# A new order table for a hand-planned attention, FFT and FFN kernel on one core

## The chip, the cores and the metric

The kernel runs on one core of a Trainium2 chip. Its engines are TensorE (PE; its weight loads stand apart as PEld), VectorE (DVE), ScalarE (ACT), GpSimd (POOL) and SyncE (SP), which here issues nearly all DMAs. The metric is device time in microseconds, the median over runs.

## The reference

```python
scores = scale * np.matmul(q, k.transpose(0, 1, 3, 2))      # B, H, S, D = 8, 8, 576, 64
mask = (rel >= 0) & (rel < 64)
scores = np.where(mask, scores, -1000000000.0)
attn = softmax(scores)                                      # over the last axis
x = (attn @ v), heads side by side                          # B, 576, 512
mixed = np.real(np.fft.fft(np.fft.fft(x, axis=1), axis=2))
u = x + mixed
un = (u - mean) / np.sqrt(var + 1e-06)
out = u + np.maximum(un @ w_ch1, 0.0) @ w_ch2               # 512 -> 2048 -> 512
```

All inputs and both weights are drawn in numpy; the weights arrive in 64-bit floats.

## The kernel before

The 4608 rows are cut into 36 tiles `T` of 128 rows. Tiles 0 to 10 do attention in fp32 (`whole`), the later ones in pairs of fp16 numbers, high and low part, with three products in place of one (`PASSES`). For each tile there is one score step (L652, into `psc`, 64 by 64 blocks of TensorE, 32 matmuls in fp32 and 48 of 128 columns in fp16) and two steps for attention times values (`av`, L729, into `pa`, blocks of 128 by 64, one for each half `g` of the heads). All other matmuls use the whole array of 128 by 128, or nearly all of it. VectorE masks the scores (L667), ScalarE takes the exponentials (L675), GpSimd or VectorE inverts the sums (L742, L744), VectorE scales the result (L748).

For each of the 8 batches a Fourier transform follows (`flip_y` L832, `dstage` L972, `sstage` L1006); its rows go to DRAM and are fetched again, tile by tile, by an indirect DMA (`gather`, into `mt`). `norm_tile` adds, normalises and turns the tile.

The FFN works on 18 chunks `c` of two tiles. Chunk 0 runs in fp32 while the weights are still being converted (three VectorE instructions a piece, L1219, L1224, L1231; 32 pieces). Chunks 1 to 13 have 16 first steps (`one`, L1330, 12 matmuls of 256 columns into `ph`) and 16 second steps (`go`, called second step below, L1311, 6 matmuls of 512 columns into `po`); between them ScalarE makes the high part `hh` (L1339) and VectorE the low part (L1342). Chunks 14 to 17 use a scheme with seven products in place of eight (`ffn7`, L1484 and L1459); the last one ends with `direct` (L1471).

Nothing is scheduled by a compiler. Each piece of work is registered as an `Op` in a `Plan`, which numbers them from 0 to 3200. `ORDER` is a table of these numbers, written out; the ops are emitted in that order, and each engine, and SP's queue of DMAs too, runs its own in the order in which they were emitted. `SECOND` lists the ops that go to their second engine where there is a choice of two. `Plan.follow` walks the table with modelled durations. What of that walk reaches the chip is the engine of each op and the length of the modelled gaps: ahead of FFN chunk 0, a TensorE gap over `WARM[0]` is filled with matmuls on nothing (`warm`, L1658), to keep its clock up:

```python
if early and o.eng == "PE" and gap > WARM[0]:
    for _ in range(int((gap - WARM[1]) / 0.21)):
        nc.tensor.matmul(warm, wide[:, 0:P], wide, start=True, stop=True)
```

Of the 8 banks of PSUM, `ph` has a ring of two, `po` has one of two, and a ring of four (`ps`) serves the scores (two banks a step), `av` (one a step), the turns and the stages of the transform.

Of the kernel before, what the change touches and what calls it, by code (L numbers as in the profile page):

```python
# [48 lines left out]
SLACK = 0.5  # L49
PLAIN = 1  # L50
WSC, PSC = 1.1, 1.0
# [222 lines left out]


class Op:
    __slots__ = ("eng", "dur", "lat", "fn", "deps", "outs", "prio", "wait", "ready", "allocs", "bufs", "idx", "durs", "margin", "port", "slack")


class Plan:  # L280
# [16 lines left out]
    def op(self, eng, dur, prio, fn, reads=(), writes=(), lat=0.0, alt=(), holds=(), port=True):  # L297
# [3 lines left out]
        o = Op()  # L301
# [5 lines left out]
        deps = set()  # L307
# [85 lines left out]
def attn_fft_ffn_kernel(ctx: ExitStack, tc: tile.TileContext, q, k, v, w1, w2, gidx, dft_d, dft_s, mask, out):  # L393
# [1040 lines left out]
    def ffn7(c):  # L1434
# [145 lines left out]
        if end:  # L1580
# [18 lines left out]
            for k, n in enumerate((2, 3)):  # L1599
                w, z = slice(CH * k, CH * k + CH), Buf()  # L1600
                o = op("DVE", 0.36, -11, lambda n=n, k=k: add(x_(0)[:, k], n, x_(0)[:, k]), [bpo[2], Bosc, ba], [z], port=False)
                if k == 0:
                    o.deps.discard(right_half)
# [86 lines left out]
```

## Time and profile before

| | |
|---|---|
| median of 3 runs | 971.66 us |
| lowest and highest | 968.44 and 972.33 us |
| the profiled execution | 967.56 us |
| its span, first to last instruction | 965.8 us |
| TensorE busy | 941.5 us, 97% |
| VectorE, ScalarE, GpSimd busy | 688.9, 427.3 and 455.7 us |
| mean granted TensorE clock | 1.000 |

TensorE's busy time is the union of the matmuls' spans from start to modelled end. A 512-column matmul is shown with 380 ns, though the next one can start well before that; so the pace of TensorE is read from starts, not from busy time.

### The profile page before, as it was taken

Reading aid. Unit: us, or ns where it says so; the run is one execution under the profiler, and the core shown is the slowest. Engines: PE = TensorE matmul, PEld = TensorE weight load, DVE = VectorE, ACT = ScalarE, POOL = GpSimd, SP = SyncE. Lnnn points to the kernel's source line nnn. Section 1 sums busy time; section 2 is a strip of 40 time slices with the busy share of each in tenths; the row PEclk is TensorE's granted clock in tenths of the full one; section 3 lists DMA queues with packets and bytes.
Section 4 is the critical chain, followed back from the end, with each engine's and each line's share of the span. In section 5 each row is a group of like instructions: output and inputs, shape, how many; then the busy total and the mean of one; then the engine's idle time right before and its main releaser. Section 6 shows DMA issues by size and latency. Waiting matters only on the chain.

```text
span 965.8 us, 24609 instructions
## 1 busy us (share of the span) xinstructions
PE 941.5 (97%) x9646; PEld 688.5 (71%) x9646; DVE 688.9 (71%) x1940; ACT 427.3 (44%) x1010; POOL 455.7 (47%) x866
## 2 busy tenths in 40 slices
PE   7889999999999999999999999999999999999998
PEld 5666767666676677666676667766576668888887
DVE  6998998886866676666655765666588998566645
ACT  5876676655443524442334333343343634223311
POOL 3664342474663343866734435364863524333251
PEclk9999999999999999999999999999999999999999
DMA  9986734779779765896566855586543511101101
GB/s 234 224 234 195 208 98 108 126 138 184 135 137 164 121 116 130 166 164 105 116 128 140 154 116 107 127 169 127 95 106 89 118 23 37 44 12 45 45 1 67
DMA packets 293892, 117.14 MB, mean 121 GB/s; under 512 B 277064, under 2 KB 277448, under 8 KB 293776
## 3 DMA queue, kind: packets, MB, share of 16 engines
q1 hardware_dynamic: 290912, 106.52, 52.9%
q0 software_dynamic: 2720, 8.92, 3.3%
q8 instruction: 76, 1.25, 0.6%
q14 instruction: 40, 0.33, 0.1%
q10 hardware_dynamic: 144, 0.13, 0.0%
HBM read 54.99 MB, written 14.17 MB: 72 GB/s over the span
## 4 chain that ended last, share of the span: by engine, by line
PE 74%; DMA 9%; DVE 8%; POOL 5%; issue 2%; ACT 1%; SPq 1%; DVEq 0%; POOLq 0%; ACTq 0%
PE po L1311 24%; PE ph L1330 23%; PE ph L1484 9%; PE po L1459 7%; PE pa L729 3%; PE pz L1006 2%; PE pg L972 2%; DMA py<-yp 2%; DMA uhl<-up 2%; PE psc L652 2%; DMA mt<-md,gix 2%; DVE pr L667 1%; POOL flex L508 1%; DMA qn<-in_q 1%; POOL y L508 1%
## 5 line engine op out<-in xcount | busy, mean ns | idle before, releaser
L1311 PE MATMUL po<-w1s,hh 128*128 128x512 f16 (+1 forms) x1312 | 334.9, 391 | 1.9 <-DVE hh L1342 1.9
L1330 PE MATMUL ph<-uhl,w0s 128*128 128x256 f16 (+1 forms) x2616 | 331.9, 278 | 2.6 <-DVE hh L1342 2.4
L1330 PEld LDWEIGHTS <-w0s 128*128 128x128 f16 x2496 | 241.7, 98 | 62.4 <-issue 3.9
L1311 PEld LDWEIGHTS <-hh 128*128 128x128 f16 x1248 | 117.7, 98 | 107.5 <-DVE hh L1342 4.2
L1339 ACT ACTIVATE hh<-ph 128x512 f16<-128x512 f32 x104 | 61.6, 592 | 146.4 <-PE ph L1330 119.1
L1342 DVE SCALAR_TENSOR_TENSOR hh<-ph,hh 128x512 f16<-128x512 f32 x104 | 71.3, 686 | 45.3 <-ACT hh L1339 44.9
L675 ACT ACTIVATE pr<-pr,nm 128x128 f32<-128x128 f32 x288 | 90.8, 390 | 27.9 <-DVE nm L667 26.6
L742 POOL TENSOR_TENSOR rc<-rc,mone 128x4 f32<-128x4 f32 x43 | 49.7, 1158 | 104.4 <-ACT rc L735 56.6
L1484 PE MATMUL ph<-uhl,w0s 128*128 128x256 f16 x768 | 90.2, 273 | 0.0
L1484 PEld LDWEIGHTS <-w0s 128*128 128x128 f16 x768 | 75.0, 98 | 9.5
L1080 POOL DMA_INDIRECT mt<-md,gix x34 | 40.5, 1193 | 75.9 <-DVE mv L1108 55.4
L667 DVE CUSTOM_DVE_ANT_0 pr<-psc,mskb 128x128 f32<-128x128 f32 x288 | 64.9, 285 | 10.5 <-PE psc L652 10.1
L508 POOL TENSOR_TENSOR flex<-pr,flex 128x128 f16<-128x128 f32 x92 | 45.6, 524 | 23.1 <-ACT flex L498 16.8
L1495 ACT ACTIVATE hx<-ph 128x512 f32<-128x512 f32 x31 | 18.4, 597 | 68.2 <-PE ph L1484 52.7
L1459 PEld LDWEIGHTS <-hh 128*128 128x128 f16 x434 | 42.4, 98 | 4.9
L729 PE MATMUL pa<-ve,pt 128*64 128x65 f16 (+1 forms) x776 | 42.4, 204 | 3.0 <-ACT pt L498 1.2
L1508 POOL TENSOR_TENSOR hl<-hx,hh 128x256 f16<-128x256 f32 (+1 forms) x40 | 25.8, 674 | 41.0 <-ACT hh L498 22.2
L508 POOL TENSOR_TENSOR up<-un,up 128x128 f16<-128x128 f32 x60 | 28.4, 502 | 31.2 <-ACT up L498 21.2
L729 PE MATMUL pa<-va,pt 128*64 128x65 f16 (+1 forms) x776 | 42.4, 204 | 0.0
L508 POOL TENSOR_TENSOR y<-xu 128x128 f32<-128x128 f32 x76 | 37.6, 524 | 9.9 <-DVE xu L748 6.6
L1105 DVE CUSTOM_DVE_ANT_0 xu<-xu,mt 128x511 f32<-128x511 f32 (+6 forms) x50 | 35.2, 703 | 9.5 <-DMA mt<-md,gix 9.3
L1115 ACT ACTIVATE un<-xu,mv 128x512 f32<-128x512 f32 x34 | 24.4, 717 | 36.1 <-DVE mv L1108 26.7
(229 smaller groups left out, 1633.4 us busy)
## 6 DMA issues: line engine op xcount, KB each, us to landing
wd<-in_moe_w_ch SPq DMA_DIRECT2D x20, 512.0 KB
out<-xu SPq DMA_DIRECT2D x35, 256.0 KB
kn<-in_k SPq DMA_DIRECT2D x32, 256.0 KB
qn<-in_q SPq DMA_DIRECT2D x32, 256.0 KB
flex<-in_moe_w_ch SPq DMA_DIRECT2D x12, 512.0 KB
ve<-va SPq DMA_DIRECT2D x47, 130.0 KB
flex<-in_v SPq DMA_DIRECT2D x22, 256.0 KB
md<-mp SPq DMA_DIRECT2D x24, 192.0 KB
```

The source lines that it names most:

```text
L508: eng.tensor_tensor(out=out[:, k : k + w], in0=in0[:, k : k + w], in1=in1[:, k : k + w], op=al)
L667: nc.vector.tensor_tensor_reduce(out=t["pr", g][:, hp], in0=t["ps", g][:, hp], in1=mskb[:, m : m + P], scale=-0.125, scalar=3.0e38, op0=AL ...
L675: nc.scalar.activation(pr, pr, AF.Exp, bias=t["nm", g][:, hp : hp + 1], scale=-1.0)
L729: nc.tensor.matmul(pa[sl, hp], pt[:, sl], v_, start=(x == 0), stop=(x == len(mm) - 1))
L742: eng.tensor_tensor(out=rc, in0=rc, in1=mone, op=ALU.pow)
L1080: nc.gpsimd.indirect_dma_start(out=mts[T], out_offset=None, in_=mds[pb][0 : HR if n < 4 else 2 * HR], in_offset=bass.IndirectOffsetOnAxis( ...
L1311: nc.tensor.matmul(t["po"][i], l_, r_, start=(f == 0 and x == 0), stop=(f == NKF - 1 and x == len(mm) - 1))
L1330: nc.tensor.matmul(ph, l_, r_, start=(x == 0), stop=(x == len(mm) - 1))
L1339: nc.scalar.activation(t["hh", j][:, 0], ph, AF.Relu)
L1342: nc.vector.scalar_tensor_tensor(out=hh[:, 1], in0=ph, scalar=0.0, in1=hh[:, 0], op0=ALU.max, op1=ALU.subtract)
L1459: nc.tensor.matmul(t["po", bk][:, x], t["h", j][a][:, slot], right(n, j, b_), start=(j == 0 and k == 0 and n in opens), stop=(j == seven - ...
L1484: nc.tensor.matmul(ph, l_, r_, start=(x == 0), stop=(x == len(mm) - 1))
```

## The change

`ORDER` and `SECOND` are replaced; both tables were made with other settings of the plan. The plan's op gets a `mode` (2 for the score step, 1 for `av`, 0 for all else), and where the mode of a TensorE op differs from that of the one before it, `MODE` = 0.1 us is added to its modelled time. The modelled times of the score and `av` steps are changed. FFN chunks 1 to 13 are planned with `FSLACK`, which assumes that what they wait for comes later than modelled, by 0.4 times the `LATE` of the producer's engine. One dependency that had been dropped by hand in the last chunk (the first half of the last sum against `right_half`) is kept again. No op is added, removed or altered in what it computes. The opening stretch of the new table, which is the attention up to FFN chunk 0 and a little beyond, follows an older order: it starts with the loads of keys and queries, and the weight pieces come later in SP's queue.

```diff
-SLACK = 0.5
+SLACK, FSLACK = 0.5, 0.4
...
-WSC, PSC = 1.1, 1.0
+WSC, PSC = 0.95, 0.7
...
 ORDER = [int(i) for i in """
-11 171 172 3 16 1 0 10 2 7 9 12 13 14 174 175 176 177 180 185 8 186 187 17 181 182 200 18 203 204 188 201 205 206 183
...
+    MODE = 0.1
...
-        o.port, o.slack = port, self.slack
+        o.port, o.slack, o.mode = port, self.slack, mode
...
-        port = 0.0
+        port, mode = 0.0, 0
...
-                end = self.pe_time(busy, st, o.dur)
+                end = self.pe_time(busy, st, o.dur + (self.MODE if o.mode != mode else 0.0))
+                mode = o.mode
...
-        op("PE", WSC if whole else PSC, base + 2, lambda: score((0, 1)), rd, [*bss, *bps])
+        op("PE", WSC if whole else PSC, base + 2, lambda: score((0, 1)), rd, [*bss, *bps], mode=2)
...
-            op("PE", 0.63 if whole else 0.5, base + 6 + 0.5 * g, av, rd, [bpa, bx] if g == 0 else [bpa])
+            op("PE", 0.65 if whole else 0.43, base + 6 + 0.5 * g, av, rd, [bpa, bx] if g == 0 else [bpa], mode=1)
...
-                right_half = op("PE", 0.66, pr + 13.2, lambda: direct(0, 1), rd, [bpo[2]])
+                op("PE", 0.66, pr + 13.2, lambda: direct(0, 1), rd, [bpo[2]])
...
-                if k == 0:
-                    o.deps.discard(right_half)
...
-    plan.slack = 0.0
+    plan.slack = FSLACK
     for c in range(PLAIN, SEVEN):
         ffn(c)
```

## Rows read from the trace of the kernel before

**Rows 1.** The page: granted TensorE clock in 40 slices of the span, in tenths.
```profile
PEclk9999999999999999999999999999999999999999
```

**Rows 2.** Busy time of each engine in four stretches; the second number is their length.
```profile
0.00:97.00 97.00, 82.54 (x964) 61.31 (x965) 81.27 (x287) 68.35 (x180) 49.80 (x97) 1.00 0.84 221
97.00:157.00 60.00, 60.00 (x416) 41.57 (x415) 54.26 (x135) 43.28 (x110) 21.85 (x40) 1.00 0.57 148
157.00:788.00 631.00, 625.36 (x6675) 433.19 (x6674) 441.79 (x1272) 267.57 (x636) 321.72 (x626) 1.00 0.65 128
788.00:965.80 177.80, 173.60 (x1597) 152.39 (x1595) 111.62 (x248) 48.10 (x88) 62.31 (x106) 1.00 0.12 34
```

**Rows 3.** TensorE's waits from 157 us on: us in total, times, longest.
```profile
PE ph L1330 <- DVE hh L1342: 2.4, 3, 1.0
PE po L1311 <- DVE hh L1342: 1.9, 3, 0.8
PE pa L729 <- DMA pt<-flex: 0.9, 3, 0.3
```

**Rows 4.** Timeline of TensorE around one `av` step: start, us, what.
```profile
399.92 1.48 PE L1330 MATMUL ph<-uhl,w0s 128*128 128x256 f16 x12
401.23 1.46 PE L1311 MATMUL po<-w1s,hh 128*128 128x512 f16 x6
402.62 0.22 PE L729 MATMUL pa<-ve,pt 128*64 128x65 f16 x1
...
402.99 0.20 PE L729 MATMUL pa<-ve,pt 128*64 128x65 f16 x1
...
403.13 1.47 PE L1311 MATMUL po<-w1s,hh 128*128 128x512 f16 x6
404.43 0.82 PE L1330 MATMUL ph<-uhl,w0s 128*128 128x256 f16 x6
```

**Rows 5.** Timeline of TensorE around a score step among FFN steps.
```profile
433.38 0.86 PE L652 MATMUL psc<-kst,qbd 64*64 64x128 f16 x48
434.18 0.39 PE L1311 MATMUL po<-w1s,hh 128*128 128x512 f16 x1
```

**Rows 6.** Timeline of TensorE around a score step with an `av` step behind it.
```profile
460.94 0.86 PE L652 MATMUL psc<-kst,qbd 64*64 64x128 f16 x48
461.74 0.22 PE L729 MATMUL pa<-ve,pt 128*64 128x65 f16 x1
...
462.24 0.61 PE L1311 MATMUL po<-w1s,hh 128*128 128x512 f16 x2
```

**Rows 7.** Busy time of the filling matmuls (L1658) in the opening: TensorE, weight loads.
```profile
0.00:97.00 97.00, 14.33 (x84) 8.88 (x84) 1.00 0.84 221
```

**Rows 8.** The chain that ended last, one link near the opening's end: start, us.
```profile
83.72 6.69 DMA mt<-md,gix
```

**Rows 9.** VectorE's groups up to 97 us: busy us, mean ns, idle before.
```profile
L1224 DVE SCALAR_TENSOR_TENSOR w0s<-wd,w0s 128x512 int32<-128x512 int32 x9 | 6.5, 722 | 0.2
...
L1219 DVE TENSOR_SCALAR w0s<-wd 128x512 int32<-128x512 int32 x9 | 6.0, 680 | 4.9 <-DMA wd<-in_moe_w_ch 4.9
...
L744 DVE RECIPROCAL rc<-rc 128x4 f32<-128x4 f32 x6 | 1.1, 176 | 0.2
```

**Rows 10.** The page's group of GpSimd's inverses.
```profile
L742 POOL TENSOR_TENSOR rc<-rc,mone 128x4 f32<-128x4 f32 x43 | 49.7, 1158 | 104.4 <-ACT rc L735 56.6
```

**Rows 11.** Timeline of TensorE around one wait of a second step.
```profile
698.84 0.59 PE L1311 MATMUL po<-w1s,hh 128*128 128x512 f16 x2
700.24 1.04 PE L1311 MATMUL po<-w1s,hh 128*128 128x512 f16 x4 [0.81 <-DVE hh L1342]
```

**Rows 12.** Timeline of VectorE near the end.
```profile
959.73 0.69 DVE L508 TENSOR_TENSOR xu<-xu,s 128x512 f32<-128x512 f32 x1
...
960.53 0.88 DVE L1559 SCALAR_TENSOR_TENSOR xu<-po,osc,xu 128x256 f32<-128x256 f32 x2
```

More of the change, by code (lines that the diff above doesn't have):

```diff
@@ L276 @@
 class Op:
-    __slots__ = ("eng", "dur", "lat", "fn", "deps", "outs", "prio", "wait", "ready", "allocs", "bufs", "idx", "durs", "margin", "port", "slack")
+    __slots__ = ("eng", "dur", "lat", "fn", "deps", "outs", "prio", "wait", "ready", "allocs", "bufs", "idx", "durs", "margin", "port", "slack", "mode")
 class Plan:
@@ L295, in __init__, with op @@
         self.slack = 0.0
-    def op(self, eng, dur, prio, fn, reads=(), writes=(), lat=0.0, alt=(), holds=(), port=True):
+    def op(self, eng, dur, prio, fn, reads=(), writes=(), lat=0.0, alt=(), holds=(), port=True, mode=0):
         o = Op()
         o.durs = {e: d + self.FIXED[e] for e, d in ([(eng, dur), alt[:2]] if alt else [(eng, dur)])}
-        o.port, o.slack = port, self.slack
+        o.port, o.slack, o.mode = port, self.slack, mode
         o.margin = alt[2] if len(alt) > 2 else self.MARGIN
@@ L1600, in ffn7 @@
                 w, z = slice(CH * k, CH * k + CH), Buf()
-                o = op("DVE", 0.36, -11, lambda n=n, k=k: add(x_(0)[:, k], n, x_(0)[:, k]), [bpo[2], Bosc, ba], [z], port=False)
-                if k == 0:
-                    o.deps.discard(right_half)
+                op("DVE", 0.36, -11, lambda n=n, k=k: add(x_(0)[:, k], n, x_(0)[:, k]), [bpo[2], Bosc, ba], [z], port=False)
                 put = lambda e, w=w: e.dma_start(of[P * 2 * c : P * (2 * c + 1), w], xts[2 * c][:, w])
```

277 rows, old and new, of tables (ORDER, SECOND) are left out of this document.

## Prediction

> **What bounds the kernel now.** I read the clock first, then busy time by stretch, then the waits, and last the timeline around single steps. The granted clock is 1.00 in every slice, the upper of the two levels [rows 1], so clock plays no part. The stretches [rows 2] part the run in two. Up to 97 us TensorE is idle for 97 − 82.5 = 14.5 us and fills 84 matmuls on nothing [rows 7]; at the pace of a 256-column matmul, 1.31 us for twelve or 0.109 us each [rows 4], these are 9.2 us, so at least 23.7 us of the opening hold none of the kernel's products. VectorE is busy for 81.3 of 97 us there and the DMA engines for 0.84 of it: the opening is bound by supply. From 97 us on TensorE is idle for 5.6 us until 788 and for 4.2 us after it, and the last of these is the final result's way out. Each matmul there starts when the one before lets it: six of 512 columns take 404.43 − 403.13 = 1.30 us, 0.217 each [rows 4]. So past 97 us only three things can make the kernel shorter: fewer matmuls (none is removed), fewer late starts, and less time lost between matmuls of different block shape.
>
> That loss is the point of the change, and busy time hides it; starts show it. In [rows 4] six second-step matmuls begin at 401.23, and at 0.217 the next one is due at 402.53. It is an `av` matmul and starts at 402.62: 0.09 us lost on entry. The twelve pairs of `av` start every 0.034 us (402.62 to 402.99 in eleven steps), so a follower would be due at 403.02; the next second step starts at 403.13: 0.11 us lost on leaving. The score step alone takes 434.18 − 433.38 = 0.80 us to its follower [rows 5]. With an `av` step right behind it takes the same, 461.74 − 460.94 = 0.80, and that `av` step 462.24 − 461.74 = 0.50, as after an FFN step, where it takes 0.51 [rows 4, 6]. So a direct change from score to `av` costs what leaving to full blocks costs, and saves the entry.
>
> **The changes of shape, counted.** I resolved both tables into TensorE's 781 ops and counted neighbours of unlike mode: 199 before, 143 after. Up to the first step of FFN chunk 1 there are 48 and 46, which I leave at nothing: supply covers them there. Behind it there are 151 and 97. Before, 75 blocks of narrow work (49 of one `av`, 24 of one score, one pair of `av`, one score with `av`); after, 41 (11 pairs of `av`, 10 scores alone, 10 of two `av` and a score, 5 single `av`, 5 score with one `av`). Of narrow blocks that is 34 less: 34 entries at 0.09 = 3.1 us, 34 exits at 0.105 = 3.6 us gained, and 14 more direct changes at 0.10 = 1.4 us lost: 5.3 us gained in all. Seven of the 15 direct changes go from `av` to score, which no undisturbed row shows. From below they could cost nothing (+0.7 us gain), from above an exit and an entry, 0.20 (−0.7 us). I take 0.10, as for the other direction, and keep 4.6 to 6.0. As TensorE streams without pause there, the whole sum should reach the end.
>
> [...]
>
> **Settings of the plan.** `MODE`, `FSLACK`, and the modelled durations reach the chip only through the tables and the number of fillers. The fillers lie before FFN chunk 0, where they use time in which TensorE waits anyway; a wrong number costs 0.109 each when the wait is shorter than planned. I count nothing, and for ten more or fewer ±1 us, which goes into the opening's bounds.
>
> **Late starts behind 157 us,** where FFN chunk 1 begins. TensorE's waits on `hh` are 4.3 us in six, on the turned probabilities 0.9 us in three [rows 3]. The idle time is counted from a modelled end: in [rows 11] the third matmul was due at 698.84 + 2 × 0.217 = 699.27 and came at 700.24, 0.97 us late where 0.81 is shown. With 0.16 more for each of nine the loss is 6.6 us. The new table assumes `hh` to come 0.4 × 0.5 = 0.2 us later, so the same six events would cost 1.2 us less. The shortest distance of TensorE work between an FFN first step and the second step that reads it rises from 1.7 to 2.0 us. Against it: by my count along the tables, places where a PSUM bank of `ps` is taken again within 4 us of TensorE work after its last filling rise from 1 to 7, and first steps with one step of 1.3 us between them and the user of their bank from 1 to 4; that first one was not late before. As all other starts are drawn anew I take 1.0 us gained, with bounds of 4 us either way: 4 is most of the 6.6, and as much again could come up.
>
> **The opening.** Two things move. First, keys and queries go ahead of the first weight piece in SP's queue (which becomes the seventh DMA). The first score step can then start earlier, but VectorE, which sits idle for 4.9 us until that piece lands [rows 9], does its three conversions, about 2 us at 0.7 each, later. I set one against the other. Second, what VectorE has in its queue ahead of the normalised second tile, which opens the FFN: 41 weight conversions before, 37 after, at 0.72 us each [rows 9] 2.9 us less. But six more inverses are on VectorE ahead of it, at 0.18 us [rows 9] 1.1 us. Net 1.8 us, of which I take 1.4 as VectorE is busy for 81.3 of 97 us [rows 2]. DMAs issued ahead of the FFN are as many. The link that ends the opening, a gather of 6.7 us [rows 8], hangs on SP's queue, which I can't follow to the microsecond: bounds 4 us earlier, 4 us later.
>
> **The end.** The dependency kept again lets the first half of the last sum wait for `right_half`. In the trace that sum starts at 960.53, and VectorE was busy with the add before it until 960.42 [rows 12], so the freedom gave nothing, and I count nothing; if that add were gone, it would cost one half sum, 0.4 us.
>
> **Sum.** 5.3 + 1.0 + 1.4 = 7.7 us off the profiled execution's 967.56, 959.9. That execution lies 4.1 us below the median of 971.66, so for a median 964.0.
>
> **The rivals.**
> - *The opening gives it back (no change).* The older order puts the weight pieces six or more DMAs later. If FFN chunk 0 or the gather behind it comes 6 us later, 5.3 + 1.0 − 6 leaves 971.4. For it: the opening is bound by supply, DMA share 0.84 [rows 2]. Against: the conversions ahead of the FFN are fewer. 0.23.
> - *Narrow blocks wait for banks (slower).* Two `av` steps and a score take all four banks of `ps`; the following user of `ps` waits until a bank is read, and all of TensorE behind it. A bank of `av` is held by an inverse of 1.16 us on GpSimd [rows 10] and the scaling behind it. From 0.13 us for each of the 41 blocks the 5.3 us are gone; from (7.7 + 4.9)/41 = 0.31 us the kernel is slower by 0.5%. At 0.4 us, 16.4 − 7.7 = 8.7 us, 980.4. Against: the waits behind 157 us are on `hh` and on the turned probabilities, none on the reading of a bank of scores or of `av` [rows 3]. 0.09. [...]
> - *The new order suits the chip better in all three parts.* Late starts fall by 4 us and the opening by 4: 971.7 − 13.3 = 958.4. 0.13.
> - *Merged steps keep part of the loss.* Each step, not each block, may pay its run-out, so that only the entries are saved: 3.1 + 2.4 = 5.5 us, 966.2. For it: no undisturbed row shows two `av` steps in a row. Against: the twelve pairs inside a step pay nothing [rows 4]. 0.03.
>
> **How the numbers follow.** The forecast has 0.52. Within it the bounds of each part, not all at one end, give 960.5 to 968. What a measurement of this kernel can tell from no change is about 0.5%, 4.9 us, so "faster" is below 966.8: 0.45 of the forecast's 0.52, 0.13 of the third rival, 0.02 of the last, 0.60. Slower: the bank rival, with 0.01 of a worse opening, 0.10. The rest, 0.30, is the same. The range reaches from 957 (all good bounds) to 971.5 (the opening gives it back); what lies beyond is below 0.2.
>
> **What would show it.** In the profile after: blocks of two or three narrow steps in TensorE's timeline, the entry and exit still 0.09 and 0.11; no matmul more or less in L652, L729, L1330, L1311; waits on `hh` at or below 4.3 us; the first fp16 first step of chunk 1 some 1.4 us earlier than now, and from there to the last matmul about 6 us less. I am wrong if a direct change from `av` to score costs far more than 0.2, if waits on PSUM banks or on the turned probabilities show up behind the blocks, or if chunk 1 starts several us later than in the trace of before.

## The result and the profile after

| | before | after |
|---|---|---|
| median (4 runs each) | 970.17 us | 957.97 us |
| lowest and highest | 968.44 and 972.33 us | 954.84 and 959.15 us |
| the profiled execution | 967.56 us | 959.15 us |
| its span | 965.8 us | 957.4 us |

The ratio is 0.9868, with a 95% interval of 0.9834 to 0.9902: faster, by 12.2 us between the medians and by 8.4 us between the profiled executions. Three of the four times before are those of the table ahead of the prediction. The execution profiled before lies below all four, and the one profiled after is the highest of its four, so the two traces show less of the gain than the medians do.

The page of the new kernel, busy time of each engine and the granted clock in 40 slices:

```profile
PE 931.4 (97%) x9638; PEld 689.9 (72%) x9638; DVE 692.5 (72%) x1960; ACT 431.5 (45%) x1013; POOL 446.9 (47%) x835
...
PEclk9999999999999999999999999999999999999999
```

The granted clock is at 0.9 or more in every slice, as in [rows 1], and 1.00 in each stretch below, as in [rows 2]; it has no part in the difference. Busy time of each engine in the stretches of [rows 2]; the second number is their length:

```profile
0.00:97.00 97.00, 82.21 (x1001) 63.64 (x1002) 82.30 (x302) 71.01 (x180) 47.14 (x92) 1.00 0.84 223
97.00:157.00 60.00, 60.00 (x412) 42.34 (x408) 54.64 (x135) 43.06 (x112) 27.42 (x48) 1.00 0.55 147
157.00:788.00 631.00, 624.89 (x6713) 438.62 (x6712) 451.34 (x1286) 266.13 (x636) 316.35 (x605) 1.00 0.65 128
788.00:957.40 169.40, 164.29 (x1524) 145.26 (x1522) 104.25 (x240) 51.30 (x87) 55.96 (x91) 1.00 0.13 36
```

Beside [rows 2] the reader sees no busy share move: 624.89 for 625.36 us of the long stretch. What moved is how much was done in it: 6713 matmuls for 6675 there, 1001 for 964 up to 97 us, though the opening has fewer fillers, 76 for the 84 of [rows 7]:

```profile
0.00:97.00 97.00, 12.93 (x76) 8.10 (x76) 1.00 0.84 223
```

TensorE's waits from 157 us on (us in total, times, longest), as [rows 3] of before:

```profile
PE po L1313 <- DVE hh L1344: 1.8, 1, 1.8
PE pa L731 <- DVE nm L669: 0.8, 1, 0.8
PE py L834 <- DVE y L510: 0.7, 1, 0.7
PE ph L1332 <- DVE hh L1344: 0.7, 1, 0.7
PE pz L1008 <- DVE g L984: 0.6, 1, 0.6
PE pa L731 <- DVE xu L750: 0.5, 1, 0.5
```

The waits on `hh` fell from 4.3 to 2.5 us. Two of the others are new in kind: `av` waits for VectorE to mask scores (`nm`) or to scale an earlier `av` (`xu`). `av` reads neither; it needs a bank of the ring `ps` that they are still reading. The timeline of TensorE shows these waits, and the blocks:

```profile
153.87 1.47 PE L1332 MATMUL ph<-uhl,w0s 128*128 128x256 f16 x12
...
321.18 0.86 PE L654 MATMUL psc<-kst,qbd 64*64 64x128 f16 x48
321.97 0.22 PE L731 MATMUL pa<-ve,pt 128*64 128x65 f16 x1
...
323.09 0.19 PE L731 MATMUL pa<-ve,pt 128*64 128x65 f16 x1 [0.55 <-DVE xu L750]
...
502.31 1.04 PE L1332 MATMUL ph<-uhl,w0s 128*128 128x256 f16 x8
503.27 0.86 PE L654 MATMUL psc<-kst,qbd 64*64 64x128 f16 x48
504.07 0.22 PE L731 MATMUL pa<-ve,pt 128*64 128x65 f16 x1
...
504.82 0.19 PE L731 MATMUL pa<-ve,pt 128*64 128x65 f16 x1
504.95 0.82 PE L1313 MATMUL po<-w1s,hh 128*128 128x512 f16 x3
...
526.87 0.86 PE L654 MATMUL psc<-kst,qbd 64*64 64x128 f16 x48
528.53 0.22 PE L731 MATMUL pa<-ve,pt 128*64 128x65 f16 x1 [0.79 <-DVE nm L669]
...
721.76 0.19 PE L731 MATMUL pa<-ve,pt 128*64 128x65 f16 x1
721.88 0.86 PE L654 MATMUL psc<-kst,qbd 64*64 64x128 f16 x48
```

The block at 503.27 is the change at its best: a score step, then two `av` steps. The eight matmuls ahead are due to end their turn at 502.31 + 8 × 0.109 = 503.18, and the score comes at 503.27: 0.09 lost on entry. It takes 0.80 to its follower, as in [rows 5, 6]. The 24 pairs of both `av` steps start in 504.82 − 504.07 = 0.75 us, 0.033 apart, so the second step of the two pays nothing; the exit takes 0.13, of which 0.10 is loss. At 721.76 the one direction that before didn't show, `av` to score, takes 0.12 from start to start where 0.03 is usual: 0.09 lost. At 321.97 and 526.87 the same kind of block is held up, once by a bank of `av`, once by a bank of scores.

VectorE at both ends of the run (the first row is the first masking, at 9.74 us before):

```profile
8.47 0.29 DVE L669 CUSTOM_DVE_ANT_0 pr<-psc,mskb 128x128 f32<-128x128 f32 x1 [2.36 <-PE psc L654]
...
951.13 0.88 DVE L1561 SCALAR_TENSOR_TENSOR xu<-po,osc,xu 128x256 f32<-128x256 f32 x2 [0.84 <-PE po L1473]
...
952.49 0.75 DVE L1576 SCALAR_TENSOR_TENSOR xu<-po,osc,xu 128x512 f32<-128x512 f32 x1 [0.49 <-PE po L1473]
```

The last half sums wait for the matmuls (0.84 us) and no longer stand behind an add, as in [rows 12].

**Where the 8.4 us came from.** For each pair of matmuls that follow each other I took the distance of their starts and subtracted the usual distance for the first one's shape. At a change of shape what is left over, up to 0.14 us, is the change's loss and more is a late start; elsewhere what exceeds 0.1 us is one. "Products" is the sum of the usual distances, and "rest" holds gaps below 0.1 us and the time to the first matmul. By that, up to the start of the last matmul (961.22 us before, 952.01 after):

```
                       before   after   difference
products               893.5    893.5      0.0
fillers                  9.2      8.3     -0.9
changes of shape        22.1     16.5     -5.6
late starts, to 210 us  23.5     21.7     -1.8
late starts behind       7.3      8.0     +0.7
rest                     5.6      4.0     -1.6
from there to the end    4.55     5.36    +0.8
```

Chunk 1's first step starts at 153.87 for 156.81 us, 2.9 earlier; from it to the last matmul 798.1 us pass for 804.4, 6.3 less. About 0.9 us of that is work which moved: eight turns of keys that stood behind chunk 0's start now stand ahead of it, and about as much, most of it of a transform, moved from behind chunk 1's start to ahead of it. Behind chunk 1's start the 151 changes took 16.2 us, the 97 take 10.6: 0.107 and 0.109 each.

### The profile page after: what moved, and what is told of

Its sections match the earlier page's. It is cut to its first block, busy times and chain, and to the rows that moved or that the text cites. A ratio compares the mean times of both kernels' runs of the same rounds, so it can differ in the third digit from the quotient of the medians.

```text
span 957.4 us, 24610 instructions
## 1 busy us (share of the span) xinstructions
PE 931.4 (97%) x9638; PEld 689.9 (72%) x9638; DVE 692.5 (72%) x1960; ACT 431.5 (45%) x1013; POOL 446.9 (47%) x835
## 4 chain that ended last, share of the span: by engine, by line
PE 83%; DVE 5%; DMA 4%; POOL 4%; issue 2%; ACT 1%; SPq 0%; POOLq 0%; DVEq 0%; ACTq 0%
PE ph L1332 28%; PE po L1313 27%; PE ph L1486 9%; PE po L1461 7%; PE pa L731 3%; PE pz L1008 2%; PE psc L654 2%; PE pg L974 2%; DMA qn<-in_q 2%; POOL h L510 1%; DVE y L510 1%; PE py L834 1%; DMA flex<-in_v 1%; PE mt L1051 1%; POOL flex L510 1%
## 5 line engine op out<-in xcount | busy, mean ns | idle before, releaser
L1313 PEld LDWEIGHTS <-hh 128*128 128x128 f16 x1248 | 119.8, 98 | 107.4 <-DVE hh L1344 2.8
L1082 POOL DMA_INDIRECT mt<-md,gix x34 | 38.4, 1128 | 80.1 <-DVE mv L1110 41.0
L744 POOL TENSOR_TENSOR rc<-rc,mone 128x4 f32<-128x4 f32 x38 | 43.6, 1152 | 53.8 <-ACT rc L737 51.4
L510 POOL TENSOR_TENSOR up<-un,up 128x128 f16<-128x128 f32 x76 | 35.8, 501 | 48.0 <-ACT up L500 37.6
L1502 DVE TENSOR_TENSOR hx<-hx 128x128 f32<-128x128 f32 x104 | 28.0, 312 | 31.9 <-ACT hx L1497 30.9
L510 POOL TENSOR_TENSOR flex<-kn,flex 128x128 f16<-128x128 f32 x72 | 36.8, 540 | 29.9 <-ACT flex L500 27.0
L1461 PEld LDWEIGHTS <-hh 128*128 128x128 f16 x434 | 42.5, 98 | 4.9
L731 PE MATMUL pa<-ve,pt 128*64 128x65 f16 (+1 forms) x776 | 39.0, 203 | 4.3 <-ACT pt L500 1.9
L510 POOL TENSOR_TENSOR flex<-qn,flex 128x128 f16<-128x128 f32 x76 | 34.5, 483 | 16.9 <-ACT flex L500 8.2
L510 POOL TENSOR_TENSOR flex<-pr,flex 128x128 f16<-128x128 f32 x68 | 34.6, 538 | 14.8 <-ACT flex L500 8.6
```

Of the source, the lines that this page charges most:

```text
L510: eng.tensor_tensor(out=out[:, k : k + w], in0=in0[:, k : k + w], in1=in1[:, k : k + w], op=al)
L731: nc.tensor.matmul(pa[sl, hp], pt[:, sl], v_, start=(x == 0), stop=(x == len(mm) - 1))
L744: eng.tensor_tensor(out=rc, in0=rc, in1=mone, op=ALU.pow)
L1082: nc.gpsimd.indirect_dma_start(out=mts[T], out_offset=None, in_=mds[pb][0 : HR if n < 4 else 2 * HR], in_offset=bass.IndirectOffsetOnAxis( ...
L1313: nc.tensor.matmul(t["po"][i], l_, r_, start=(f == 0 and x == 0), stop=(f == NKF - 1 and x == len(mm) - 1))
L1461: nc.tensor.matmul(t["po", bk][:, x], t["h", j][a][:, slot], right(n, j, b_), start=(j == 0 and k == 0 and n in opens), stop=(j == seven - ...
```

## The experiments

An edit of the table is written as a rule on lists; OLD and NEW are the two tables, and of `SECOND` each op keeps the choice of the table that it comes from. All ratios are to the kernel before on the same chip, with a 95% interval.

### One opening with the other rest

The cut lies at the first step of chunk 1 (about 155 us). First the old opening with the new rest, `e1_old_opening`:

```diff
-ORDER = NEW
+ORDER = OLD[:661] + [i for i in NEW if i not in OLD[:661]]
```

> The opening of the table before (all ops up to the first FFN step of chunk 1) with the rest in the new order; 48 changes of block shape in the opening and 97 behind it. Theory (the gain sits behind chunk 1's first step, most of it in the 54 changes saved): FFN chunk 1 starts where it did before, within 1 us of 156.8, and the rest takes about 5.5 us less, so some 5 to 8 us below before, ratio 0.992 to 0.995. Rival (the opening makes the gain): 0 to 3 us below before, ratio 0.997 to 1.000.

Then the new opening with the old rest, `e2_new_opening`:

```diff
-ORDER = OLD
+ORDER = NEW[:662] + [i for i in OLD if i not in NEW[:662]]
```

> The new opening with the rest in the order before; 46 changes of shape in the opening and 151 behind it. Theory: chunk 1 starts about 2.9 us earlier than before and the rest takes as long as before, so 2 to 4 us below before, ratio 0.996 to 0.998. Rival (the opening makes the gain): 8 us or more below before, ratio 0.992 or less.

Measured: 964.78 us and a ratio of 0.9963 (0.9948 to 0.9977) with the old opening, 970.70 and 1.0030 (1.0014 to 1.0045) with the new one. The first lies between its theory (up to 0.995) and its rival (from 0.997), the second above both of its own; neither half brings its share alone. In the first, chunk 1 starts at 160.24 us, 3.4 later than before: 1.3 us of the products now stand ahead of it, and one step of a transform comes late. From there to the last matmul 798.5 us pass, about what the new table takes (798.1). In the second, chunk 1 starts at 153.2 us, 3.6 ahead of before, and 12 us later the lead is gone at one place behind the cut. TensorE's waits from 150 to 175 us, in the first and in the second:

```profile
PE pz L988 <- DVE g L964: 1.6, 1, 1.6
```

```profile
PE ph L1312 <- DVE hh L1324: 5.0, 1, 5.0
```

The last 0.6 us of that wait and what stands behind it, as in [rows 2]:

```profile
164.90:168.30 3.40, 2.77 (x13) 1.87 (x13) 3.37 (x14) 2.87 (x9) 1.43 (x4) 0.50 0.00 0
```

The granted clock is 0.50 there, for 1.00 in [rows 2], and the 13 matmuls take about 1.4 us more than at the usual distances. The cut itself costs more than what was to be measured; that the work in flight across it was planned by neither table is the likely reason, and was not tried. So these two runs price no opening; they show that one table's opening doesn't fit the other's rest at this place. The changes cost the same in both: 9.9 us for 90 behind 210 us, 14.9 for 139.

### The same cut later

At op 880, about 209 us, behind the first chunk in fp16. The old opening with the new rest, `e6_old_opening_late_cut`, the new one with the old rest, `e7_new_opening_late_cut`, and the new kernel itself again, `e5_new_again`:

```diff
-ORDER = NEW
+ORDER = OLD[:880] + [i for i in NEW if i not in OLD[:880]]
```

> The order before for its first 880 ops (up to a second step of FFN chunk 2, about 209 us), the new order behind; at that place the two tables have done the same work but for 10 ops, so the seam should cost little. Theory (opening 2.9 us, changes 5.6 us): it loses the new opening's 2.9 us and 5 of the 54 saved changes, so 3 to 4 us slower than the new kernel, ratio to before 0.990 to 0.992. Rival (the first old-opening mix lost its time through the order, not the seam): ratio 0.995 or more, as that one.

```diff
-ORDER = OLD
+ORDER = NEW[:880] + [i for i in OLD if i not in NEW[:880]]
```

> The new order for its first 880 ops, the order before behind. Theory: the mix of the first series lost 6.2 us at one first step right at its seam; without that, the new opening alone gives 2 to 4 us, ratio 0.996 to 0.998. Rival (the new opening gives nothing, or its lead is eaten by late starts behind it): ratio 0.999 to 1.003.

> The new kernel unchanged, on the same chip as the three others, against the kernel before. Expected ratio 0.987 (0.984 to 0.990); in its trace 97 changes of shape behind chunk 1's start at about 0.11 us each, and the late starts of 0.1 us and more sum to 6 to 10 us, about half of them in the same places as in the first trace.

| opening | rest | median us | ratio | first second step of chunk 2 | changes behind 210 us | late behind 210 us |
|---|---|---|---|---|---|---|
| old | old | 968.11 | 1 | 210.3 | 138: 14.8 us | 7.3 us |
| old | new (e6) | 966.20 | 0.9978 (0.9962 to 0.9994) | 209.8 | 88: 9.7 us | 11.3 us |
| new | old (e7) | 960.33 | 0.9927 (0.9909 to 0.9945) | 205.6 | 136: 14.5 us | 5.0 us |
| new | new (e5) | 955.05 | 0.9862 (0.9843 to 0.9880) | 204.7 | 88: 9.6 us | 8.2 us |

The last three columns come from the profiled executions. e5's ratio came out as expected; e6 has its rival's number and e7 gains more than its theory and its rival had. The new opening is worth 7.8 us with the old rest, the new rest 5.3 us behind the new opening and 1.9 behind the old one. In the traces the rest's changes take 5 us less in both, as the count says. In e6 4.0 us of that return as late starts, the largest at one bank of scores (TensorE's waits from 210 us on):

```profile
PE pa L711 <- DVE nm L649: 2.5, 1, 2.5
PE ph L1312 <- DVE hh L1324: 1.4, 2, 1.2
```

The wait of 2.5 us ends at 221.43, and 1.5 us behind it the granted clock is 0.50 (as in [rows 2]):

```profile
222.90:229.70 6.80, 5.63 (x28) 3.74 (x27) 5.78 (x15) 2.33 (x5) 1.21 (x4) 0.50 0.36 82
```

In these 6.8 us matmuls start up to twice as far apart as at a clock of 1.00 (256 columns: 0.20 us in the 24 from 224.97 us on, for 0.109 in [rows 4]), which comes to about 2.5 us; the count above books them as late starts. So more than half of the 4.0 us is a clock of 0.50 behind one wait. Of e6's twelve executions the two with a mean granted clock of 1.000 took 962.86 us both, 3.3 below the median. In these runs the rest's gain came whole only behind the opening that it was planned with. How much of e6's other late starts belongs to the cut itself is not settled.

### Taking the blocks apart, and packing without a plan

In `e3_split_blocks` 36 FFN steps of the new table are moved one place earlier on TensorE, in between the narrow steps of a block, which takes the changes behind chunk 1's start from 97 to 139:

```diff
-..., second, score, av, one, ...
+..., second, score, one, av, ...
```

> The new table with 36 narrow steps of its packed blocks parted again by an FFN step that is moved one place earlier: 139 changes of shape behind chunk 1's start in place of 97, all else as in the new table. Theory (each change costs 0.10 us on TensorE and nothing hides it): 42 x 0.10 = 4.2 us more than the new table, so the stretch from chunk 1's first step to the last matmul takes 802.3 us against 798.1, and the time lies 8 us below before, ratio about 0.992. Rival (the gain comes from the replanned order, and changes of shape are hidden): within 1 us of the new table, ratio 0.987.

Measured: 963.78 us, ratio 0.9962 (0.9945 to 0.9979), 8.7 us above the new kernel's 955.05 in another job. The changes behind chunk 1's start took 14.9 us, 0.107 each, 4.3 more than with 97. Late starts behind 210 us came to 13.0 us, 4.8 more than in e5, in a profiled execution that is the slowest of its ten; from chunk 1's first step to the last matmul it takes 808.0 us, where the theory had 802.3. The price of a change is confirmed, and the rival that changes are hidden fell; the other half of the loss is late starts that came up with the moved steps; what each of them hangs on was not tried.

In `e4_packed_before` 23 narrow steps of the old table are moved past up to four FFN steps to meet another, and nothing else is planned anew, so the changes fall from 151 to 120:

```diff
-..., score, one, second, av, ...
+..., score, av, one, second, ...
```

> The table before with 23 narrow steps moved next to another one, past up to four FFN steps: 120 changes of shape behind chunk 1's start in place of 151, nothing else replanned. Theory: 31 x 0.10 = 3.1 us less lost at changes; late starts may grow by 0 to 3 us since the moved steps were not replanned, so 0 to 3 us below before, ratio 0.997 to 1.000, with the loss at changes in the trace 3.1 us lower. Rival (packing makes narrow blocks wait for PSUM banks): the loss at changes falls but waits of 0.3 us and more stand behind the packed blocks, ratio above 1.000.

Measured: 980.41 us, ratio 1.0135 (1.0107 to 1.0163). The changes took 13.1 us, 3.1 less than before, as their count says; but 22.4 us are late behind 210 us, 15 more. TensorE's waits from 157 us on:

```profile
PE pa L709 <- DMA pt<-flex: 8.7, 3, 5.2
PE po L1291 <- DVE hh L1322: 2.3, 2, 2.0
PE pa L709 <- DVE nm L647: 2.0, 2, 1.4
PE ph L1310 <- DVE hh L1322: 1.2, 2, 1.0
```

An `av` that is moved forward to its neighbour arrives before its turned probabilities (8.7 us in three waits, [rows 3] had 0.9) and before its bank is free. Two of these three waits, of 5.2 us until 328.41 and of 2.6 until 682.41, have a granted clock of 0.51 and 0.50 in and behind them:

```profile
325.20:332.10 6.90, 3.69 (x32) 1.91 (x33) 1.47 (x4) 1.66 (x3) 1.58 (x4) 0.51 0.74 141
683.70:687.10 3.40, 3.40 (x13) 1.62 (x11) 1.40 (x2) 1.62 (x3) 0.84 (x2) 0.50 0.94 189
```

The matmuls of these stretches take about 3.7 us more than at the usual distances, a quarter of the 15 us. The executions bear it out: with a mean granted clock of 0.997 they took 977.68 and 979.20 us, with 0.991 and 0.992 984.62 and 983.12. Fewer changes are thus worth their price each only in an order where all that feeds the blocks is in time. The rival of waiting banks is real as a mechanism (2.0 us on `nm`), and most of this loss is of another kind.

### Late starts one by one

`e8_late_starts` takes the new table and moves seven small groups: two low parts of `hh` ahead of other VectorE work in its queue, a turn and two transform stages behind the work that they waited for, and `av` ahead of score in three blocks that waited for a bank.

```diff
-..., stats T24, ..., hh low c10 j5, ...
+..., hh low c10 j5, stats T24, ...
...
-..., score T27, av T26, ...
+..., av T26, score T27, ...
```

> The new table with seven small moves, each at a place where its trace shows TensorE 0.7 to 2.0 us late: two VectorE ops that make the low part of hh go ahead of an op that waits for a gather or for GpSimd, one turn and one pair of transform stages go behind the next steps, and in three blocks av goes ahead of the score. Those places sum to 7.0 us. Theory (a late start comes from one op's place in a queue): 2 to 6 us below the new kernel, ratio to before 0.981 to 0.985. Rival (late starts only move to the next place): within 1 us of the new kernel, 0.987.

Measured: 957.22 us, ratio 0.9886 (0.9862 to 0.9910), no better than 955.05 for the new table in the same job. Late starts behind 210 us were 9.0 us for 8.2. TensorE's waits from 157 us on:

```profile
PE ph L1312 <- DVE hh L1324: 3.7, 3, 1.6
PE pz L988 <- DVE nm L649: 1.0, 1, 1.0
PE pa L711 <- DMA pt<-flex: 1.0, 1, 1.0
```

The places that were treated are gone from the list and others have come. The theory that each late start hangs on its local place in a queue fell; its rival, that late starts only move, fits.

### What makes the opening shorter

The prediction set the earlier loads against the later conversions. `e9_loads_first` makes that one edit in the old table: the first two weight pieces go behind the keys and queries of tiles 0 and 1 in SP's queue, and their conversions behind the masking of tile 0 on VectorE. Other than in the new table, the values of tile 0 stay behind the weight pieces.

```diff
-11 171 172 3 16 1 0 10 2 7 9 12 13 14 174 175 176 177 180 185 8 186 187 17 181 182 200 18 203 204 188 201 205 206 183
+171 172 3 1 0 10 2 7 9 174 175 176 177 180 185 8 186 187 181 182 200 203 204 188 201 11 16 205 206 12
+13 14 183 184 17 18 21 22 23 173 178 209 24 179 210 214 193 19 230 234 229 189 190 191 211 212 26 194 195 235
...
```

> The table of before with one edit in its first forty ops: SP's queue starts with the keys, the queries and the mask of tile 0 and the keys and queries of tile 1, and the first two weight pieces follow behind these; on VectorE their conversions stand behind the masking of tile 0 in place of ahead of it. All else as before. Theory A (the opening's lead is made by the order of the first loads, and is passed on whole): the first masking starts about 2 us earlier than before's 9.7 us, the first FFN step of chunk 0 about 2 us earlier than 82.3 us, and the kernel takes 2 us less than before, ratio 0.998. Theory B (as predicted: what the loads give, the conversions that come later on VectorE take back; the lead comes from fewer conversions ahead of the FFN): the first masking is as early, but the first FFN step of chunk 0 is within 0.7 us of 82.3, and the ratio is 1.000.

`e10_weights_first` makes the opposite edit in the new table, with `e11_control` beside it.

```diff
-..., ldK T0, ..., ldQ T0, ..., ldmask, ldV T0, flipK T0, ..., wload 0.0, ..., conv 0.0, ..., wload 0.1, ...
+wload 0.0, ..., ldK T0, ..., ldQ T0, ..., ldmask, wload 0.1, ldV T0, conv 0.0, flipK T0, ...
```

> The new table with the opposite edit: the first weight piece leads SP's queue and the second stands behind the mask, as in the table of before, and the three conversions of the first piece stand ahead of tile 0 on VectorE. All else as in the new table. Theory A: the first masking starts at about 9.7 us in place of 7.7, the first FFN step of chunk 0 about 2 us later than the control's, and the kernel takes about 2 us more than the control. Theory B: the first FFN step of chunk 0 and the time are within 0.7 us of the control's.

> The new kernel unaltered, as the control of this job: 13 us less than before, ratio 0.986, the first masking at 7.7 to 8.5 us, the first FFN step of chunk 0 at 78.5 to 80.2 us, that of chunk 1 at 152.1 to 153.9 us, by both theories.

The 82.3 us in the expectations is the second of the two first steps at the head of chunk 0; before, the very first matmul of chunk 0 starts at 80.44 us.

| profiled execution | first score | first `av` | chunk 0 | chunk 1 | median us | ratio |
|---|---|---|---|---|---|---|
| before | 8.57 | 15.51 | 80.44 | 156.81 | 967.94 | 1 |
| e9 (old, loads first) | 6.77 | 16.82 | 82.81 | 158.68 | 975.06 | 1.0079 (1.0064 to 1.0095) |
| e10 (new, weights first) | 8.59 | 16.45 | 82.05 | 155.74 | 956.39 | 0.9875 (0.9858 to 0.9893) |
| e11 (new) | 6.58 | 13.99 | 80.22 | 153.89 | 956.42 | 0.9879 (0.9860 to 0.9898) |

In e9 the first score comes 1.8 us earlier and the first `av` 1.3 later: neither theory foresaw it. The reason stands in ScalarE's timeline, where the values are copied as soon as they land, before and in e9:

```profile
14.79 1.27 ACT L498 COPY ve<-va 64x520 f32<-64x520 f32 x2 [1.12 <-DMA va<-in_v]
```

```profile
16.06 1.27 ACT L478 COPY ve<-va 64x520 f32<-64x520 f32 x2 [4.20 <-DMA va<-in_v]
```

and in SP's queue in e9:

```profile
6.54 1.71 SPq L1190 DMA_DIRECT2D wd<-in_moe_w_ch  x3
8.29 0.67 SPq L508 DMA_DIRECT2D va<-in_v  x1
```

The values are issued at 8.29 us, 1 us earlier than before (9.27), and land 1.3 later. The same loads stand ahead of them in both: three weight pieces, keys and queries of two tiles, and the mask. What differs is the time in which SP waits for a buffer of the keys before it can issue those of tile 1. Before, a weight piece is under way then; in e9 the DMA engines have next to nothing to move (last two numbers: their share and GB/s; before, then e9):

```profile
4.50:6.50 2.00, 2.00 (x12) 1.39 (x11) 1.51 (x3) 0.00 (x0) 0.00 (x0) 1.00 1.31 256
```

```profile
4.50:6.50 2.00, 1.81 (x13) 1.47 (x11) 0.00 (x0) 0.95 (x2) 0.00 (x0) 1.00 0.05 9
```

At before's 256 GB/s these 2 us are worth 0.5 MB, as much as one weight piece (512 KB). The new table issues the values ahead of any weight piece, at 2.88 us, and has its first `av` at 13.9, 13.7 and 14.0 us in three executions. With the weights put first again (e10) all of the opening up to chunk 1 is 1.9 us later in the trace than in e11's. That is about what executions of the new kernel differ by there (1.8 us), and e11's own opening lost time to a granted clock of 0.50 twice, from 39.0 to 42.4 and from 52.7 to 56.1 us. Both edits change the number of fillers too, as the modelled gaps change: 107 for 84 in e9, 91 for 76 in e10. The medians don't show a loss in e10, 956.39 for 956.42 us of four runs each that spread over 4 and 3 us, so a loss of 2 us is neither shown nor excluded, and neither theory is settled. In e9 the 1.9 us at chunk 1 grew to 4.3 at the last matmul (965.53), in an execution that is the lowest of its six; between the medians it is 7.1. So an order that met its work late lost more behind.

## Why the prediction was right, point by point

**The direction and the main term were right.** The changes of shape gave 5.6 us for 5.3. Entry 0.09, exit 0.10 and direct change 0.09 to 0.10 stand in the trace as counted, steps of one shape that follow each other inside a block pay nothing, so the rival by which merged steps keep part of the loss is refuted. The price was 0.107 to 0.109 us a change behind 210 us with 88, 110, 126 and 138 changes (after, e4, e3, before), which makes it a price per change and no accident of one table.

**The opening was the term that was mis-sized.** It was put at 1.4 us, all of it ahead of chunk 0. Chunk 1 starts 2.9, 4.7 and 2.9 us earlier in three executions of the new kernel (after, e5, e11), inside the bounds of 4 or just beyond. The step that failed is that the stretch from chunk 0's first matmul to chunk 1's was put at nothing: its changes of shape as covered by supply, its late starts because they were counted from 157 us on only. It takes 73.7 us in all three, and in e3, e7, e8 and e10 as well, for 75.9 to 76.4 in before, e4, e6 and e9, with as much work in it. That is 2.2 to 2.7 us, the larger part of the lead. By the rule of the table above, with the median distance of each shape as the usual one, about 2 of them are late starts (3.0 before, 1.1 after), and four changes fewer are worth 0.4; e10 has it with the weights first, so the order of the first loads doesn't make it. What of the new `ORDER` or of the new `SECOND` does is not shown; no run parts the two.

Ahead of chunk 0, loads were set against conversions ("I set one against the other"). The first `av` comes 1.5 to 1.8 us earlier in all three. At chunk 0's first matmul (80.17, 78.45 and 80.22 for 80.44, with 0.9 us more of products ahead of it) 0.3, 2.0 and 0.2 of that is left, so part of the lead is lost on the way in two of three; in e11 the clock of 0.50, twice for 3.4 us, took part of it. Whether conversions take it back, and what fewer conversions give, no run shows. By the times, e7 gives the new opening 7.8 us with the old rest. In its trace 4.7 us of that are the lead at 206 us and 2.3 fewer late starts behind it. That the opening gives the gain back is refuted.

**Late starts behind chunk 1 had the wrong sign in two of three profiles.** The forecast was 1.0 us less. The waits on `hh` did fall, from 4.3 to 2.5, but the total was 8.0, 8.2 and 6.4 us in three executions, for 7.3 before. Waits on banks being read took the place: 1.3 us in the profile after (0.8 on `nm`, 0.5 on `xu`), 0.03 us for each of 41 blocks, far below the 0.13 at which this rival would have cancelled the gain. That the stretch behind chunk 1's start shortened by the 6.3 us that were added up for it (5.3 and 1.0) is luck: it is 5.6 of changes, 0.9 of work moved ahead and some small gaps, with 0.7 of late starts against them.

**The end** was counted at nothing. The half sum no longer stands behind the add of [rows 12], but waits for TensorE. From the last matmul's start to the end 5.4 us pass for 4.6; in e5 and e11 it is 4.6 again, so the order alone doesn't make it longer.

**The sum against its own time** came close by luck: 959.9 us predicted for a profiled execution, 959.15 measured, because the miss in the opening, the late starts, the 1.6 us of small gaps and the longer end offset each other, and because the execution profiled is the highest of its four. In the traces of e5 and e11 the span is 954.9 us, some 11 below before. The median lies lower, 957.97 for 964.0, near the range's lower end. Of these 6 us about 4 come from the step that added 4.1 us to reach the median of three runs: in three later jobs the kernel before has medians of 967.95, 968.11 and 967.94 us (27, 17 and 11 runs), where its profiled execution lies too. Against these the new kernel is 13.1 us (e5) and 11.5 us (e11) faster, where 7.7 was forecast. No version that was tried is clearly faster than it.

## What to carry to other kernels

Count the changes of TensorE's block shape and read their price from starts, not from busy time: here 0.11 us each, for all three shapes, and here it was saved where the order was planned with it, while packing alone made the kernel 12 us slower by late starts (15 us more) and a clock of 0.50 and 0.51 in and behind two of them. Read the granted clock in every trace that holds a wait of some microseconds: what looks like many late starts can be one wait and slower matmuls behind it, as in e6, where a clock of 0.50 for 6.8 us followed a wait of 2.5. In a first stretch bound by supply, follow the first product's whole chain through the queue of loads, the last of its inputs included: one load put earlier was worth nothing here while another input landed 1.3 us later, and large pieces at the head of the queue filled 2 us in which the DMA engines otherwise had next to nothing to move (256 GB/s for 9). A table planned as a whole could not be priced by halves at either of two cuts; look for the cut's own waits first.

## What the hardware showed that was not expected

- A change between two narrow shapes (128 by 64 to 64 by 64) costs 0.09 us, about as much as one to the full array (0.10), though both use parts of the array only.
- Executions of one kernel differ in the opening: chunk 1 of the new kernel starts at 153.87, 152.14 and 153.89 us. In the first TensorE waited 3.7 us for the landing of queries up to 97 us, in the second 0.5; in the third, with 1.4, the granted clock was 0.5 for 3.4 us twice.
- In e2, e4 and e6, TensorE idled for 5.0, 5.2, 2.6 and 2.5 us, and its granted clock was 0.50 or 0.51 for 3.4 to 6.9 us, from within the wait or shortly behind it.
- A load issued 1 us earlier landed 1.3 us later, with the same loads ahead of it, when the DMA engines had moved next to nothing for 2 us (9 GB/s for 256) while the queue waited for a buffer.
